# Two groups of fp32r rounding copies moved from VectorE to ScalarE in a fused attention, token-mixing and feed-forward kernel

## The chip, the cores and the metric

The kernel runs on one core of one Trainium2 chip. The metric is the device time of one execution in microseconds. Time zero of every view of the trace is the start of the span. TensorE multiplies (PE; PEld is its weight load), VectorE is DVE, ScalarE is ACT, GpSimd is POOL, SyncE is SP and issues nearly all DMAs.

## The reference, cut to what matters

```python
B, H, S, D, d_model, d_ff = 2, 8, 768, 64, 512, 1024
# attention with 8 global and 96 local keys and a linear bias, per batch and head
x = softmax(q k^T / sqrt(D) + bias) v              # to (B, S, 512)
# mixing
theta = x @ w_theta
zr, zi = x * cos(theta), x * sin(theta)
y = einsum('ts,bsd->btd', w_tok_r, zr) + einsum('ts,bsd->btd', w_tok_i, zi)
u = x + y
x2 = u + relu(u @ w_ch)
# feed-forward with a 3-tap convolution gate
h = relu(x2 @ w_in)
out = (h * sigmoid(conv(h, conv_w))) @ w_out
```

Weights come as fp64 and are converted on the chip.

## The kernel before, in words

**The numbers.** Products behind attention are made of three fp32r matmuls. Each operand is split into a rounded copy, `hi`, of type fp32r, and the remainder, `lo`, the operand minus `hi`; then hi × hi, lo × hi and hi × lo are added up in PSUM. `Net.hi(eng, out, in_)` (L99) makes the rounded copy: with "A" an activation of type Copy on ScalarE (L101), with "P" a copy on GpSimd, with anything else a copy on VectorE (L105). `Net.lo` (L107, row L109) subtracts, on VectorE unless told "P". So `lo` reads what `hi` wrote.

**Order of the work.** The schedule is written out by hand: each engine executes its instructions in the order in which the program issues them, and an instruction that waits holds all that is queued behind it on its engine.

**Attention** (`run_fast`, L799). The loop over j has 48 pairs of query tiles (16 heads of a batch, three pairs each) and 9 more rounds that drain it. In round j TensorE makes the scores of j, ScalarE the exponentials of j - 2 (L330), TensorE the transposes of j - 3 (L339), ScalarE their evacuation for j - 4 (L101, a<-PT), TensorE the product with v for j - 5, VectorE the softmax reduction of j - 1 (L321) and every third round the normalising of a head (L274 to L276). Every sixth round a column block c of x (four blocks of 128 per batch) is complete: `transpose_x` (L430) transposes it in two halves through the one bank X, and each half is copied to `xT` (on ScalarE, but on VectorE for the last block of batch 1). Three rounds later `split_xT` (L441) makes `xTs`: `hi` of 128x768 at the end of a round, `lo` in the next one. The last block of batch 1 is transposed and split at once, in round 54 (L861). A queue of small steps (`net.run`, weight conversion: L117 on ScalarE, L122 to L130 on VectorE, then `hi` on ScalarE and `lo` on VectorE) is worked off in the rounds.

**Theta.** theta of batch 0 (six tiles of 128 rows) is multiplied inside the attention loop by `theta_0`; `reduce_theta` (L473) reads a tile from its bank on ScalarE (L477, then L478), and VectorE takes off whole turns (L480). For batch 1 tiles 0 to 3 are opened in rounds 52, 54, 55 and 56 with column blocks 0 to 2 (`theta1_open`, L461; banks TH, S, S, PT). `tail` (L620) then adds block 3, and tiles 4 and 5 follow in banks TH and S (L656 to L658), that is, in the banks of tiles 0 and 1 once their reductions have read them.

**Trig.** `trig` (L482) turns a reduced theta tile into z in stages: on ScalarE an Abs and two Sin of 128x512 (L487 to L489); on VectorE two products with x (L493); then `hi` of both z and `lo` of both z (L495 to L498). The strings `em`, `eh`, `el` say on which engine products, `hi` and `lo` run; each has a letter for the real and one for the imaginary part. `trig0` (L501) runs the six tiles of batch 0 in a staggered way, one call per round from round 52 on: call k issues the first stage of tile k, the second of tile k - 1 and the third of tile k - 2, in that order. Calls 0 to 4 come in the loop. In `tail` come, in this order (L652): the reduction of theta tile 0 of batch 1 (L477, L478), call 5, the reduction of tile 1, L480 of tile 0, call 6, L480 of tile 1, then call 7:

```python
        red = [self.reduce_theta(th[t], r[t]) for t in range(2)]
        for chain in (red[0], early, red[1], red[0], early, red[1]):
            next(chain, None)
        for _ in early:
            pass
        th += [n.bank("TH"), n.bank("S", 2)]
        for t in (4, 5):
            self.theta_part(t, th[t], range(KC))
        reduce(th[2], r[2])
        reduce(th[3], r[3])
```

**Behind that** the token products of batch 0 start (`tok`, L525, 24 matmuls of 128x384 for each of the tiles s), first with z of tile 0. The trig tiles of batch 1 (L677) already use "AA" for `hi`. Then come the channel product, the feed-forward product with its gate, and the output product.

Of the kernel before, what the change touches and what calls it, by code (L numbers as in the profile page):

```python
# [407 lines left out]
class Mix:  # L408
# [32 lines left out]
    def split_xT(self, b, c, el="V"):  # L441
        n = self.net
        h, l = self.xTs
        n.hi("V", h[:, c], self.xT[b][:, c])
        yield
        n.lo(el, l[:, c], self.xT[b][:, c], h[:, c])

# [53 lines left out]
    def trig0(self):  # L501

        n = self.net
        z, tr = [[None, None] for _ in range(NT)], []
        self.z = [z, None]
        for k in range(NT + 2):
            if k == 1:
                zs = [n.slot(f"a{i}", [P, 3, 2, DM], F32R, "z") for i in range(4)]
                for i in range(2 * NT):
                    z[i // 2][i % 2] = zs[i // 3][:, i % 3]  # L510
            if k < NT:
                tr.append(self.trig(0, k, self.r[:, k], z[k], "VV", "VV", "VV"))
            for g in tr[max(0, k - 2) :][::-1]:
                next(g)
            yield
# [510 lines left out]
```

## Time and profile before

| | us |
|---|---|
| median of 3 runs | 418.61 |
| the 3 runs | 418.59, 418.61, 419.8 |
| the profiled execution | 418.75 |
| its span, first to last instruction | 416.5 |
| outside the span | 2.25 |

Durations and starts below are those of the profiled execution. A row of the timeline gives start, duration, engine, line, operation, output and inputs, count, and in brackets an idle wait ahead of it and what ended it. A row of the groups gives line, engine, operation, output and input, shape and type, count, then busy time and mean ns of one, then idle time ahead. Two instructions of one engine can overlap a little: the next one starts before the one ahead has ended.

### The profile page before, as it was taken

How to read it: one execution, taken by the hardware profiler on the slowest of the kernel's cores; microseconds unless marked ns; L12 is line 12 of the kernel's file. 1: busy time of each engine (PE TensorE's matmuls, PEld its weight loads, DVE VectorE, ACT ScalarE, POOL GpSimd, SP SyncE). 2: the span in 40 equal slices, each digit the busy share in tenths (PEclk: the TensorE clock that was granted, in tenths of full speed). 3: DMA queues.
4: the chain of work that ended last, by engine and by line, in shares of the span. 5: the costliest groups of instructions: out<-in, count | busy, mean ns of one | idle time of the engine just before them, and what ended most of it. 6: DMA issues, size and time to landing. Idle time of an engine off the chain costs nothing.

```text
span 416.5 us, 6402 instructions
## 1 busy us (share of the span) xinstructions
PE 403.7 (97%) x2376; PEld 379.2 (91%) x2376; DVE 318.4 (76%) x733; ACT 236.8 (57%) x449; POOL 4.4 (1%) x14
## 2 busy tenths in 40 slices
PE   4899999999999999999999999999999999999995
PEld 3899999988897899999999999999999998888885
DVE  4579999667568997899999999999699999800001
ACT  2777888685669536864436245446776889300000
POOL 4000000000000000000000000000000000000000
PEclk9999999999999999999999999999999999999999
DMA  6965776441420004006564352221000000111111
GB/s 168 255 177 178 214 226 161 123 131 35 142 84 2 0 9 144 2 1 188 178 202 155 101 169 84 63 91 52 0 2 0 2 0 0 53 49 50 52 50 58
DMA packets 13095, 38.03 MB, mean 91 GB/s; under 512 B 1856, under 2 KB 2304, under 8 KB 13056
## 3 DMA queue, kind: packets, MB, share of 16 engines
q1 hardware_dynamic: 12816, 37.13, 29.3%
q10 hardware_dynamic: 240, 0.41, 0.4%
q8 instruction: 20, 0.33, 0.3%
q14 instruction: 19, 0.16, 0.1%
HBM read 34.39 MB, written 3.15 MB: 90 GB/s over the span
## 4 chain that ended last, share of the span: by engine, by line
PE 95%; DMA 3%; DVE 1%; SPq 0%; issue 0%; DVEq 0%
PE O L112 26%; PE S L112 26%; PE PT L112 16%; PE TH L112 13%; PE X L112 9%; PE PT L339 4%; DMA qk<-qk 2%; PE X L437 1%; DMA words<-n 1%; SPq L258 0%; DVE a L321 0%; DVE xT L105 0%; SPq L224 0%; SPq L230 0%; DVE scratch L105 0%
## 5 line engine op out<-in xcount | busy, mean ns | idle before, releaser
L112 PE MATMUL S<-qk 128*128 128x256 f32 (+1 forms) x192 | 48.7, 380 | 7.4 <-DMA qk<-qk 7.2
L330 ACT ACTIVATE a<-a,nm 128x256 f32<-128x256 f32 (+1 forms) x96 | 41.5, 482 | 10.4 <-DVE nm L321 10.4
L321 DVE CUSTOM_DVE_ANT_0 a<-S,a 128x256 f32<-128x256 f32 (+1 forms) x96 | 34.5, 399 | 14.4 <-PE PT L339 12.3
L112 PEld LDWEIGHTS S<-qk 128*128 128x128 f32 x192 | 32.6, 198 | 11.1 <-issue 7.6
L101 ACT ACTIVATE a<-PT 128x512 f32<-128x512 f32 (+1 forms) x48 | 26.6, 554 | 11.2 <-PE PT L339 10.8
L112 PE MATMUL O<-a,a 128*128 128x65 f32 x236 | 29.8, 268 | 0.0
L112 PEld LDWEIGHTS O<-a,a 128*128 128x128 f32 x236 | 28.8, 192 | 0.0
L112 PE MATMUL PT<-wt,z 128*128 128x384 f32 x144 | 28.1, 335 | 0.0
L339 PE MATMUL PT<-ident,a 128*128 128x128 f32 x176 | 27.1, 273 | 0.0
L112 PE MATMUL O<-wt,z 128*128 128x384 f32 x144 | 26.9, 334 | 0.0
L339 PEld LDWEIGHTS PT<-ident,a 128*128 128x128 f32 x176 | 22.2, 141 | 4.5
L112 PE MATMUL S<-wt,z 128*128 128x384 f32 x144 | 26.2, 335 | 0.0
L101 ACT ACTIVATE wt<-wbit 128x384 fp32r<-128x384 f32 x24 | 12.5, 521 | 23.9 <-DVE wbit L130 23.9
L112 PE MATMUL TH<-wth,xTs 128*128 128x512 f32 x96 | 25.9, 406 | 0.0
L112 PEld LDWEIGHTS PT<-wt,z 128*128 128x128 f32 x144 | 25.3, 188 | 0.0
L112 PEld LDWEIGHTS O<-wt,z 128*128 128x128 f32 x144 | 25.2, 188 | 0.1
L112 PEld LDWEIGHTS S<-wt,z 128*128 128x128 f32 x144 | 25.2, 188 | 0.0
L117 ACT ACTIVATE wbit<-wst 128x384 f32<-128x384 f32 (+1 forms) x33 | 20.2, 612 | 3.3 <-DVE wout L109 1.1
L130 DVE SCALAR_TENSOR_TENSOR wbit<-wst,wbit 128x384 int32<-128x384 int32 (+1 forms) x33 | 20.6, 623 | 1.1
L129 DVE SCALAR_TENSOR_TENSOR wbit<-wst,wbit 128x384 int32<-128x384 int32 (+1 forms) x33 | 20.5, 622 | 0.9
L123 DVE TENSOR_SCALAR wbit<-wbit 128x512 int32<-128x512 int32 (+1 forms) x48 | 18.9, 394 | 1.6
L112 PEld LDWEIGHTS TH<-wth,xTs 128*128 128x128 f32 x96 | 17.1, 189 | 3.2
(180 smaller groups left out, 872.6 us busy)
## 6 DMA issues: line engine op xcount, KB each, us to landing
wst<-w_tok SPq DMA_DIRECT2D x17, 384.0 KB, 4.6
a<-v SPq DMA_DIRECT2D x16, 357.5 KB, 4.8
qk<-qk SPq DMA_DIRECT2D x14, 396.0 KB, 5.7
out<-scratch SPq DMA_DIRECT2D x11, 256.0 KB, 2.0
qk<-w_tok SPq DMA_DIRECT2D x7, 384.0 KB, 3.3
wst<-w_out SPq DMA_DIRECT2D x5, 512.0 KB, 3.4
wst<-w_theta SPq DMA_DIRECT2D x4, 512.0 KB, 7.6
qk<-w_in SPq DMA_DIRECT2D x4, 512.0 KB, 3.4
```

The costliest lines, as they stand in the source:

```text
L101: self.nc.scalar.activation(out, in_, AF.Copy)
L112: self.nc.tensor.matmul(out, l, r, start=start, stop=stop)
L117: self.nc.scalar.activation(t.bitcast(F32), w[:, 1 : w.shape[1] : 2].bitcast(F32), AF.Abs)
L123: nc.vector.tensor_scalar(t, t, 3, 0x3FFFFFFF, op0=ALU.logical_shift_left, op1=ALU.bitwise_and)
L129: nc.vector.scalar_tensor_tensor(t, lo, 29, t, op0=ALU.logical_shift_right, op1=ALU.bitwise_or)
L130: nc.vector.scalar_tensor_tensor(t, hi, -(1 << 30), t, op0=ALU.bitwise_and, op1=ALU.bitwise_or)
L321: nc.vector.tensor_tensor_reduce(sS[:, c], s["sp"][:, c], self.T[i % H][:, 256:TW] if t0 else self.T[i % H][:, 0:256], scale=-0.125, scala ...
L330: self.nc.scalar.activation(sS[:, rng[u]], sS[:, rng[u]], AF.Exp, bias=nm[:, u : u + 1], scale=-1.0)
L339: self.nc.tensor.transpose(pt[:, c], sS[:, c], net.head["ident"])
L437: self.nc.tensor.transpose(xb[:, P * jj : P * jj + P], self.xs[b][:, t, P * c : P * c + P], n.head["ident"])
```

## The change

The rounded copies of `xT` (8 of 128x768) and those of z of batch 0 (12 of 128x512) are issued on ScalarE instead of VectorE. The remainders stay on VectorE, and so does everything else; the order of issue is the same.

```diff
@@ -441,7 +441,7 @@
     def split_xT(self, b, c, el="V"):
         n = self.net
         h, l = self.xTs
-        n.hi("V", h[:, c], self.xT[b][:, c])
+        n.hi("A", h[:, c], self.xT[b][:, c])
         yield
         n.lo(el, l[:, c], self.xT[b][:, c], h[:, c])
 
@@ -509,7 +509,7 @@
                 for i in range(2 * NT):
                     z[i // 2][i % 2] = zs[i // 3][:, i % 3]
             if k < NT:
-                tr.append(self.trig(0, k, self.r[:, k], z[k], "VV", "VV", "VV"))
+                tr.append(self.trig(0, k, self.r[:, k], z[k], "VV", "AA", "VV"))
             for g in tr[max(0, k - 2) :][::-1]:
                 next(g)
             yield
```

## Rows read from the trace of the kernel before

**Rows 1.** The page's busy times and shares by engine.

```profile
PE 403.7 (97%) x2376; PEld 379.2 (91%) x2376; DVE 318.4 (76%) x733; ACT 236.8 (57%) x449; POOL 4.4 (1%) x14
```

**Rows 2.** Windows: stretch, length, busy time by engine, granted clock, DMA.

```profile
20.00:75.00 55.00, 54.85 (x416) 51.23 (x416) 50.72 (x185) 45.77 (x105) 0.00 (x0) 1.00 0.67 196
...
145.00:350.00 205.00, 205.00 (x1173) 204.19 (x1172) 192.41 (x341) 122.89 (x214) 0.00 (x0) 1.00 0.23 73
...
412.00:417.00 5.00, 0.00 (x0) 0.00 (x0) 0.22 (x1) 0.00 (x0) 0.00 (x0) 0.87 0.12 37
```

**Rows 3.** Groups by line: rounded copies on VectorE and on ScalarE.

```profile
L101 ACT ACTIVATE g<-c 128x768 fp32r<-128x768 f32 x16 | 13.3, 833 | 0.9 <-DVE c L597 0.9
...
L105 DVE CAST xTs<-xT 128x768 fp32r<-128x768 f32 x8 | 4.4, 554 | 0.0
...
L101 ACT ACTIVATE z<-r 128x512 fp32r<-128x512 f32 x6 | 3.7, 621 | 2.9 <-DVE r L493 2.9
...
L105 DVE CAST z<-r 128x512 fp32r<-128x512 f32 x6 | 2.5, 419 | 0.0
```

**Rows 4.** Timeline of ScalarE, 118 to 165 us.

```profile
120.65 0.60 ACT L101 ACTIVATE a<-PT 128x512 f32<-128x512 f32 x1 [0.22 <-PE PT L339]
121.56 0.91 ACT L330 ACTIVATE a<-a,nm 128x256 f32<-128x256 f32 x2 [0.31 <-DVE nm L321]
...
122.78 0.49 ACT L101 ACTIVATE xT<-X 128x384 f32<-128x384 f32 x1
...
125.38 0.62 ACT L487 ACTIVATE scratch<-r 128x512 f32<-128x512 f32 x1
126.01 1.28 ACT L488 ACT_TABLE_LOAD   x1
...
127.85 0.71 ACT L489 ACTIVATE scratch<-scratch,hp 128x512 f32<-128x512 f32 x1
128.46 0.62 ACT L487 ACTIVATE scratch<-r 128x512 f32<-128x512 f32 x1
...
135.04 0.71 ACT L489 ACTIVATE scratch<-scratch,hp 128x512 f32<-128x512 f32 x1
137.90 0.60 ACT L477 ACTIVATE r<-TH 128x512 f32<-128x512 f32 x1 [2.15 <-PE TH L112]
138.53 0.63 ACT L478 ACTIVATE scratch<-r 128x512 f32<-128x512 f32 x1
...
141.05 0.57 ACT L477 ACTIVATE r<-S 128x512 f32<-128x512 f32 x1
```

**Rows 5.** Timeline of TensorE, 118 to 165 us.

```profile
123.85 0.50 PE L437 MATMUL X<-ident,xs 128*128 128x128 f32 x3
...
130.31 0.55 PE L437 MATMUL X<-ident,xs 128*128 128x128 f32 x3 [0.65 <-DVE xT L105]
...
139.79 2.96 PE L112 MATMUL TH<-wth,xTs 128*128 128x512 f32 x12
142.59 2.96 PE L112 MATMUL S<-wth,xTs 128*128 128x512 f32 x12
```

**Rows 6.** Timeline of VectorE, 118 to 165 us.

```profile
128.72 0.69 DVE L493 TENSOR_TENSOR scratch<-scratch,xs 128x512 f32<-128x512 f32 x1
129.70 0.56 DVE L105 COPY xT<-X 128x384 f32<-128x384 f32 x1 [0.29 <-PE X L437]
130.90 0.56 DVE L105 COPY xT<-X 128x384 f32<-128x384 f32 x1 [0.64 <-PE X L437]
...
152.65 0.35 DVE L122 TENSOR_SCALAR wbit<-wbit 128x384 f32<-128x384 f32 x1
```

**Rows 7.** Timeline of ScalarE, 160 to 175 us: a pair of z of batch 1.

```profile
166.91 0.62 ACT L101 ACTIVATE z<-r 128x512 fp32r<-128x512 f32 x1
167.43 0.62 ACT L101 ACTIVATE z<-scratch 128x512 fp32r<-128x512 f32 x1
167.96 0.62 ACT L487 ACTIVATE scratch<-r 128x512 f32<-128x512 f32 x1
```

## The prediction

> **What bounds the kernel now.** I began with the busy shares of the page: TensorE 97%, VectorE 76%, ScalarE 57% [rows 1]. The shares say that ScalarE has room, but they are means over stages, so I went on to stretches of time. Between 145 and 350 us TensorE is busy for all 205 us [rows 2]: what delays its arrival at 145 delays the end by as much, because no gap behind it can give the time back. After that I read the three engines' timelines from 118 to 146 us, where attention ends, the early trig tiles of batch 0 run and the theta tiles of batch 1 are multiplied. The reader is to see there that ScalarE reaches the first theta reduction (L477, 137.90) after an idle wait of 2.15 us for TensorE [rows 4], and that TensorE goes from theta tile 4 (139.79) to theta tile 5 (142.59) without a gap [rows 5]. The one gap of TensorE is 0.65 us before the X transposes at 130.31, for a VectorE copy.
>
> **What moves, and its price.** VectorE loses 8 casts of 768 columns at 554 ns and 12 of 512 at 419 ns [rows 3], 9.5 us in all. On the bound that is worth at most the 0.65 us above. ScalarE gains as many copies. The same shapes and types run there already: 833 ns for 768 columns, 621 ns for 512 [rows 3]. Behind one another they start closer than that: two of 512 take 1.05 us from 166.91 to 167.96 [rows 7], which is 0.10 us less each than they last. So I count 0.73 us for a copy of 768 (0.833 less 0.10) and 1.05 us for a pair of 512. No DMA and no other queue is touched.
>
> The rows put VectorE ahead by a factor of 1.5. The Trainium skill (ScalarE: Activation LUTs, Rules for kernel authors) advises VectorE for simple element-wise operations, as up to about 3 times faster in bf16 on single-source operations. Three times VectorE's duration would be 1.26 us for a copy of 512, an estimate from that page; the four pairs counted below would add about 5 us more, and the sum would be about 427 us. The rows of this kernel's own fp32 copies decide, and the sum stays with them.
>
> **The four casts of x of batch 0** stand in the attention loop behind ScalarE's evacuation of a step. From 20 to 75 us ScalarE is busy 45.77 of 55 us [rows 2], so 9.2 us are free against 4 × 0.73 = 2.9 us. Exponentials and evacuations are issued a whole step of the loop ahead of the matmuls that read them, and the casts come six steps apart. I cost them at nothing; the cover is that step. If it failed, the price would be at most 2.9 us.
>
> **The first three casts of batch 1** fall between 119 and 126 us. Two come ahead of ScalarE's copy xT<-X at 122.78. That copy is preceded by waits of 0.22 and 0.31 us that the casts fill, and two starts that followed a wait now overlap by 0.10 us each: 2 × 0.73 - 0.53 - 0.20 = 0.73 us later, so it ends at 122.78 + 0.73 + 0.49 = 124.00. TensorE's second X transposes, at 123.85 before [rows 5], need that single bank and start at 124.04 (0.04 us is what one engine takes to follow another in these rows). That is 0.19 us lost, and ScalarE, whose last evacuation follows TensorE, comes free at 125.57 instead of 125.38 [rows 4]. The third cast takes it to 126.30.
>
> **The trig work, in order.** ScalarE's queue is strictly the program's order. The rows from 125.38 to 128.46 (3.08 us with the table load) are tile 0, and four more tiles follow to 135.65 (135.04 plus 0.71 less 0.10), 1.80 us each [rows 4]. After the change:
>
> tile 0 runs to 129.38 and tile 1 to 131.18. Now comes the fourth cast of batch 1, which needs both VectorE copies of X. The first of them stands behind the product of tile 0's second Sin. That Sin ended at 128.56 and ends 0.92 us later, at 129.48; the product, 0.69 us less 0.09, leads to a copy at 130.12 instead of 129.70 [rows 6], ended at 130.68. TensorE's X transposes go from 130.31 to 130.72, and the second copy from 130.90 to 131.31, ended at 131.87. The cast starts at 131.91: ScalarE, free at 131.18, stands for 0.73 us with all trig work queued behind it. Then: cast to 132.64, tile 2 to 134.44, rounded pair of tile 0 to 135.49, tile 3 to 137.29, pair of tile 1 to 138.34, tile 4 to 140.14, pair of tile 2 to 141.19. Each pair's products are done in time: VectorE waits for the pairs, not the reverse.
>
> **Where it reaches the bound.** The reduction L477 reads theta tile 0 out of bank TH, and theta tile 4 is written into that same bank. It starts at 141.19 instead of 137.90, lasts 0.60 us, and TensorE enters tile 4 at 141.83 instead of 139.79: 2.04 us late (0.41 us of it would have come from X anyway). Theta tile 5 takes an S bank that the next reduction (141.05 before [rows 4]) must empty. On ScalarE that one now stands behind L478 (0.63 + 0.53 us from the start of L477), the last trig tile (1.80) and the pair of tile 3 (1.05): 141.19 + 1.16 + 1.80 + 1.05 = 145.20. With 0.57 us for itself and 0.04 us, TensorE enters tile 5 at 145.81 instead of 142.59, **3.22 us late**.
>
> Behind that I add nothing. The token products need z of tile 0, whose rounded copies are made by 135.49; the later pairs have a tile of products each (24 matmuls at 205 us / 1173 [rows 2], 4.2 us of TensorE). VectorE's waits for z before the reductions go, and its weight conversion, which began at 152.65 [rows 6], starts near 152 with TensorE 3.2 us later: its slack grows.
>
> The sum against the profiled execution: 418.75 + 3.22 = 421.97 us. The median of the runs is 0.14 us lower, which gives 421.83. I predict 421.9 us.
>
> **Unknown sizes.** The wait of 0.73 us and the shift of 0.19 us hang on several handovers. At the low end both are nothing: 3.22 - 0.92 = 2.3 us, 421.0. At the high end copies do not overlap: four pairs at 1.24 instead of 1.05 and two casts at 0.83 instead of 0.73 add 0.96 us, for 422.9.
>
> **Rivals.** *First, hidden work, not slower:* L477 could start as late as 139.15 without holding TensorE (139.79 less 0.64), which is 3.50 us after ScalarE's trig work ends now. If less than that is added ahead of it, nothing is lost, and VectorE's lighter queue may return the 0.65 us before 130.31: 418.1 to 418.8 us. For it speaks ScalarE's 57% and the 2.15 us idle; against it, that I count 5.54 us of delay there (three pairs, 3.15; two casts, 1.46; the wait, 0.73; 0.19, rounded). It decides at 3.50.
>
> *Second, only the first bank counts:* if tile 5 found its S bank emptied, just the 2.04 us would stay: 420.8. Against it, the reduction at 141.05 is the one that frees that bank.
>
> *Third, the clock falls.* The granted clock is 1.00 through the busy stretches and has a mean of 0.87 only after the last matmul, when TensorE stands idle to the end [rows 2]; 0.65 us idle before 130.31 left no trace in it. The two stalls are 1.6 and 1.2 us with 2.8 us of matmuls between. If the 12 matmuls of tile 5 (2.80 us) then ran at the level of 1.2 GHz, that would cost 2.80 us more: 424.8. The Trainium skill (TensorE: Matmul & The Clock Gate, Why this matters for your kernels) says that a long enough idle gap between bursts of matmuls brings the half clock back. By that rule the gaps matter; the rows show a fall only after the end, so I give it little.
>
> *Fourth, no effect,* if the copies in fact stayed where they are or an unseen handover hid them: 418.7.
>
> **How the numbers follow.** Both banks late, 0.79; only the first bank, 0.07; clock, 0.05: all slower. Hidden work or no effect, 0.09, nearly all of it within 0.3%, since 0.65 us is 0.16%. A measurement of this kernel can tell about 0.3%, 1.26 us, from no change. So slower 0.91, same 0.07, faster 0.02. The range takes in the second rival and the bounds, with 0.3 us for runs that spread: 420.7 to 423.1.
>
> **What would show it.** Right: the copies of z and xTs stand on ScalarE; L477 for TH starts near 141; TensorE has an idle wait of about 1.6 us before theta tile 4 and of 1.2 us before tile 5, both released by ScalarE's L477; TensorE is without a gap behind; VectorE waits for ScalarE's z. Wrong: TensorE enters the token products before 147, or a new wait stands in attention or past 150, or the granted clock is below 1.00 after the stalls.

## The result, and the profile after

Seven runs of the changed kernel have a median of 421.6 us (421.23 to 424.38) against 418.75 us for seven of the kernel before. The ratio is 1.0071, 95% interval 1.0056 to 1.0087: **slower by 0.7%**, against 421.9 us predicted. The profiled execution took 421.94 us with a span of 419.7 us. One of the seven runs, at 424.38 us, had a mean granted clock of 0.993 where the others had 0.997 to 1.000; it left no trace, and the kernel before has runs like it in a later round (423.07 and 423.25 us at 0.990), so it is not put down to the change.

The page's busy times of the changed kernel, the line that answers to [rows 1]:

```profile
PE 404.7 (96%) x2376; PEld 379.5 (90%) x2376; DVE 311.6 (74%) x713; ACT 247.8 (59%) x469; POOL 4.4 (1%) x14
```

VectorE has lost its 20 casts and ScalarE has them (713 instead of 733 instructions, 469 instead of 449). TensorE's share is 96% instead of 97%; nothing else in these shares looks worse. The groups by line show that the copies cost what their models in [rows 3] cost:

```profile
L101 ACT ACTIVATE z<-r 128x512 fp32r<-128x512 f32 x12 | 7.4, 619 | 2.9 <-DVE r L493 2.9
L101 ACT ACTIVATE xTs<-xT 128x768 fp32r<-128x768 f32 x8 | 6.7, 836 | 0.6 <-DVE xT L105 0.6
```

The loss is seen in TensorE's timeline, 118 to 168 us (answering to [rows 5]):

```profile
123.73 0.55 PE L437 MATMUL X<-ident,xs 128*128 128x128 f32 x3
...
130.46 0.55 PE L437 MATMUL X<-ident,xs 128*128 128x128 f32 x3 [0.86 <-DVE xT L105]
...
141.55 3.07 PE L112 MATMUL TH<-wth,xTs 128*128 128x512 f32 x12 [1.44 <-ACT r L477]
145.53 3.08 PE L112 MATMUL S<-wth,xTs 128*128 128x512 f32 x12 [0.91 <-ACT r L477]
148.44 2.27 PE L112 MATMUL O<-wt,z 128*128 128x384 f32 x12
```

Two new waits stand ahead of theta tiles 4 and 5, and both end with ScalarE's L477, which reads the bank that TensorE is about to overwrite. The wait ahead of the second X transposes grew from 0.65 to 0.86 us. ScalarE's timeline in the same stretch (answering to [rows 4]) shows what stands in front of L477:

```profile
125.31 0.83 ACT L101 ACTIVATE xTs<-xT 128x768 fp32r<-128x768 f32 x1
...
131.64 0.85 ACT L101 ACTIVATE xTs<-xT 128x768 fp32r<-128x768 f32 x1 [0.63 <-DVE xT L105]
...
134.19 0.62 ACT L101 ACTIVATE z<-r 128x512 fp32r<-128x512 f32 x1
134.72 0.62 ACT L101 ACTIVATE z<-scratch 128x512 fp32r<-128x512 f32 x1
135.24 0.62 ACT L487 ACTIVATE scratch<-r 128x512 f32<-128x512 f32 x1
...
139.88 0.61 ACT L101 ACTIVATE z<-r 128x512 fp32r<-128x512 f32 x1
140.40 0.61 ACT L101 ACTIVATE z<-scratch 128x512 fp32r<-128x512 f32 x1
140.92 0.57 ACT L477 ACTIVATE r<-TH 128x512 f32<-128x512 f32 x1
...
144.90 0.57 ACT L477 ACTIVATE r<-S 128x512 f32<-128x512 f32 x1
```

From 125.31 to 144.90 ScalarE has one wait, the 0.63 us for the copy of X. The idle time of 2.15 us ahead of L477 [rows 4] is gone, and the engine with 59% of the span busy has become the one that TensorE waits for.

The granted clock is 1.00 through both waits, and behind 150 us TensorE has no gap, as before (windows: stretch, length, busy time by engine, granted clock, DMA):

```profile
140.00:145.00 5.00, 3.18 (x13) 2.18 (x12) 3.17 (x6) 4.94 (x10) 0.00 (x0) 1.00 0.00 0
145.00:150.00 5.00, 4.47 (x21) 3.92 (x22) 5.00 (x10) 4.91 (x10) 0.00 (x0) 1.00 0.00 0
150.00:353.00 203.00, 203.00 (x1163) 202.29 (x1162) 186.78 (x330) 121.67 (x212) 0.00 (x0) 1.00 0.24 74
```

### The profile page after: what moved, and what is told of

The parts are those of the page before. It is cut to its first block, busy times and chain, and to the rows that moved or that the text cites. A ratio compares the mean times of both kernels' runs of the same rounds, so it can differ in the third digit from the quotient of the medians.

```text
span 419.7 us, 6395 instructions
## 1 busy us (share of the span) xinstructions
PE 404.7 (96%) x2376; PEld 379.5 (90%) x2376; DVE 311.6 (74%) x713; ACT 247.8 (59%) x469; POOL 4.4 (1%) x14
## 3 DMA queue, kind: packets, MB, share of 16 engines
HBM read 34.39 MB, written 3.15 MB: 89 GB/s over the span
## 4 chain that ended last, share of the span: by engine, by line
PE 90%; ACT 4%; DMA 3%; DVE 1%; issue 1%; SPq 0%; DVEq 0%; ACTq 0%
PE O L112 25%; PE S L112 24%; PE PT L112 15%; PE TH L112 11%; PE X L112 9%; PE PT L339 4%; DMA qk<-qk 2%; PE X L437 1%; ACT z L101 1%; ACT scratch L489 1%; ACT scratch L487 1%; DMA words<-n 1%; ACT xTs L101 0%; ACT r L488 0%; ACT L488 0%
```

## The experiments

The theory: only time in ScalarE's queue ahead of the two reductions counts, and only beyond the room: 3.50 us ahead of the first, and by the same sum 3.37 us ahead of the second (142.59 - 0.61 = 141.98, less 135.65 and the 1.16 and 1.80 us that stood there already). Rival A: each moved copy costs by itself. Rival B: VectorE, which now waits for copies made elsewhere, is late. Where nothing else is said, a diff is against the changed kernel.

### Each part alone

The copies of z only:

```diff
-        n.hi("A", h[:, c], self.xT[b][:, c])
+        n.hi("V", h[:, c], self.xT[b][:, c])
```

> Only the rounded copies of z of batch 0 go to ScalarE; those of xTs stay on VectorE. Theory (ScalarE's queue ahead of the two reductions that free the banks): trig work ends 3 pairs later, 135.65 + 3.15 = 138.80, so L477 for bank TH begins 0.35 us before the 139.15 from which it would hold TensorE: no stall before theta tile 4. L477 for the S bank begins at 138.80 + 1.16 + 1.80 + 1.05 = 142.81 and ends with its handover at 143.42 instead of 142.59: one stall of 0.83 us, total 418.75 + 0.83 = 419.6 us. Rival A (each moved copy costs by itself, through its longer duration or a handover): about 12/20 of the 2.9 us, 420.5. Rival B (VectorE, waiting for ScalarE's copies, is what is late): the whole loss of z stays, 421 or more.

The copies of xTs only:

```diff
-                tr.append(self.trig(0, k, self.r[:, k], z[k], "VV", "AA", "VV"))
+                tr.append(self.trig(0, k, self.r[:, k], z[k], "VV", "VV", "VV"))
```

> Only the rounded copies of xTs go to ScalarE; those of z stay on VectorE. Theory: two casts and one wait for the copy of X, about 2.4 us, fit in front of L477 (3.50 us), so there is no stall before theta tiles 4 and 5; the gap before the second X transposes grows from 0.65 to about 0.85 us with a small slip before it, 0.1 to 0.4 us lost, and attention gains up to 0.4 us between 52 and 55 us where VectorE's casts were in the way: 418.5 to 419.0 us. Rival A (each moved copy costs by itself): about 8/20 of the 2.9 us, 419.9. The two parts alone then add up to about 0.8 us where the whole change lost 2.9.

Measured beside the kernel before (419.27 us, the median of 29 runs): z only 420.23 us, ratio 1.0028 (0.9999 to 1.0057); xTs only 418.88 us, ratio 0.9988 (0.9970 to 1.0006). The kernel before is 0.5 us slower here than the 418.75 us that the expectations start from, and the runs scatter by about as much as is asked, so the traces decide. TensorE's timeline of z only and ScalarE's reductions there:

```profile
139.99 2.96 PE L112 MATMUL TH<-wth,xTs 128*128 128x512 f32 x12
143.59 3.08 PE L112 MATMUL S<-wth,xTs 128*128 128x512 f32 x12 [0.64 <-ACT r L477]
```

```profile
138.98 0.57 ACT L477 ACTIVATE r<-TH 128x512 f32<-128x512 f32 x1
142.96 0.57 ACT L477 ACTIVATE r<-S 128x512 f32<-128x512 f32 x1
```

As the theory had it, there is no wait before tile 4 and one before tile 5. Counted from the first theta matmul of batch 0 (77.19 here, 77.02 before), tile 5 starts at 66.40 instead of 65.57: **0.83 us late, the figure expected** (4.20 us of pairs less 3.37). With xTs only, neither tile waits (TensorE's timeline):

```profile
130.24 0.55 PE L437 MATMUL X<-ident,xs 128*128 128x128 f32 x3 [0.86 <-DVE xT L105]
...
139.73 2.96 PE L112 MATMUL TH<-wth,xTs 128*128 128x512 f32 x12
142.53 2.96 PE L112 MATMUL S<-wth,xTs 128*128 128x512 f32 x12
```

So the parts cost 0.92 and 0.36 us from the first theta matmul to the start of the last output products, 1.28 together, and the whole change costs 3.26 (table below). Rival A, a price for each copy, can't give that. Both parts draw on the same room.

### The same copies, in another order

```diff
-        for k in range(NT + 2):
+        steps = ((0,), (1, 0), (2, 1, 0), (3, 2), (4, 3), (1,), (5, 4, 2), (5, 3), (4,), (5,))
+        for k, step in enumerate(steps):
...
-        for chain in (red[0], early, red[1], red[0], early, red[1]):
+        for chain in (red[0], early, red[0], red[1], early, red[1], red[0], early, red[1]):
```

Here call k advances the tiles that `step` lists by one stage each, and the reduction is cut in three: L477, then L478, then L480 (the two ScalarE lines are 485 and 488 in this file).

> All 20 copies on ScalarE as in the change, but the order of issue at the end of attention is altered: pairs of tiles 1 and 2 come behind the first L477, and L477 of the second tile comes ahead of the last trig tile. Theory (only the place in ScalarE's queue costs): L477 for TH begins near 139.1 and ends before TensorE asks (about 140.2); the second L477 begins near 141.3, ends before 142.6: no stall before either theta tile, total 418.4 to 419.1 us, as fast as before with the same copies on the same engine. Rival A (the copies cost by themselves on ScalarE) and rival B (VectorE waits for them): 421 to 422 us as in the changed kernel.

Measured: 418.97 us, ratio 1.0002 (0.9976 to 1.0028), where the changed kernel has 1.0071. ScalarE's timeline and TensorE's:

```profile
138.85 0.58 ACT L485 ACTIVATE r<-TH 128x512 f32<-128x512 f32 x1
139.32 0.62 ACT L101 ACTIVATE z<-r 128x512 fp32r<-128x512 f32 x1
139.84 0.63 ACT L101 ACTIVATE z<-scratch 128x512 fp32r<-128x512 f32 x1
140.37 0.62 ACT L488 ACTIVATE scratch<-r 128x512 f32<-128x512 f32 x1
140.88 0.59 ACT L485 ACTIVATE r<-S 128x512 f32<-128x512 f32 x1
```

```profile
139.96 2.96 PE L112 MATMUL TH<-wth,xTs 128*128 128x512 f32 x12
142.76 2.96 PE L112 MATMUL S<-wth,xTs 128*128 128x512 f32 x12
145.56 2.27 PE L112 MATMUL O<-wt,z 128*128 128x384 f32 x12
```

All 20 copies are on ScalarE, and the loss is gone: of the 3.26 us behind the first theta matmul 0.37 are left (table below), as much as the xTs copies alone cost. VectorE still waits for ScalarE's z, 5.7 us over the whole span against 5.1 in the changed kernel (waits: us in total, times, longest; the changed kernel, then this run):

```profile
DVE z L109 <- ACT z L101: 5.1, 8, 1.6
DVE z L109 <- ACT z L101: 5.7, 7, 1.6
```

This run decides against rivals A and B: what costs is the place of the copies in the queue.

### More time in the same place

```diff
         for i, s in ((1, r), (0, a)):
-            n.hi(eh[i], z[i][:, 0], s)
+            for _ in range(2 if b == 0 else 1):
+                n.hi(eh[i], z[i][:, 0], s)
```

> As the change, but each rounded copy of z of batch 0 is issued twice on ScalarE (same source, same target). Theory: three more pairs ahead of the first L477 and a fourth ahead of the second add 3 x 1.05 + 1.05 = 4.2 us to the start of theta tile 5: 421.6 + 4.2 = 425.8 us, with 3.15 us of it before theta tile 4. Rival A (the loss comes from a fixed handover for each of the tiles, not from time in the queue): under 1 us more, 422 to 422.5. Rival B (VectorE is late): the remainders are issued as often as before, 2 us more at most.

Measured: 427.6 us, ratio 1.0182 (1.0148 to 1.0217), against 425.8 expected. The queue explains it, with another price. A pair issued twice takes 2.37 us on ScalarE (139.04 to 141.41 below), not 2.10: two copies from the same source to the same target did not overlap. ScalarE's timeline:

```profile
139.04 1.28 ACT L101 ACTIVATE z<-r 128x512 fp32r<-128x512 f32 x2
140.23 1.28 ACT L101 ACTIVATE z<-scratch 128x512 fp32r<-128x512 f32 x2
141.41 0.61 ACT L487 ACTIVATE scratch<-r 128x512 f32<-128x512 f32 x1
```

That is 1.32 us more for a pair: 3.96 us for the three ahead of tile 4, 5.28 for the four ahead of tile 5. In TensorE's timeline, counted from the first theta matmul (77.50), the two tiles start at 68.70 and 74.00 where the changed kernel has 64.74 and 68.72: later by 3.96 and 5.28. A fixed handover (under 1 us more) and a late VectorE (at most 2 us more) do not give that.

```profile
146.20 5.43 PE L112 MATMUL TH<-wth,xTs 128*128 128x512 f32 x12 [5.40 <-ACT r L477]
151.50 3.07 PE L112 MATMUL S<-wth,xTs 128*128 128x512 f32 x12
```

```profile
145.00:150.00 5.00, 3.80 (x9) 3.03 (x10) 2.28 (x5) 4.87 (x10) 0.00 (x0) 0.50 0.00 0
```

Tile 4 itself took 5.30 us instead of 2.80, at a granted clock of 0.50 (the window above); it ended just as the second reduction did (150.87 + 0.58), so this cost nothing here.

### Time on ScalarE with no copy moved

The kernel before, with 6 or 10 extra copies of 512 columns ahead of the first reduction:

```diff
+        for _ in range(6):
+            n.hi("A", e[:, 0:DM], r[5])
         red = [self.reduce_theta(th[t], r[t]) for t in range(2)]
```

> The kernel before, with 6 extra 512-column copies on ScalarE ahead of the first L477 (their target is overwritten later; nothing reads them); no copy is moved and VectorE's work is the same. Theory: 6 x 0.525 = 3.15 us is under the 3.50 us of room, L477 begins at 138.80 instead of 137.90 and TensorE goes from theta tile 3 to 4 to 5 without a gap: 0 to 0.2 us slower than before. Rival A (ScalarE time in that stretch costs in proportion): 1.5 us or more slower.

> As the one with 6, but 10 extra copies, 5.25 us on ScalarE. Theory: over the room of 3.50 us by 1.75: L477 begins at 140.90, theta tile 4 at 141.54 (1.75 us late), theta tile 5 at 144.47 (1.88 us late), total 1.9 us over the kernel before, with no change at all in which engine makes which copy. Rival B (the loss of the change comes from VectorE waiting for copies made elsewhere): no loss, since VectorE waits for none of these.

Measured beside the kernel before (419.0 us, the median of 26 runs): 419.58 us with 6, ratio 1.0016 (1.0005 to 1.0027), and 423.9 us with 10, ratio 1.0099 (1.0076 to 1.0122). ScalarE's timeline with 6 and TensorE's wait:

```profile
135.20 3.94 ACT L101 ACTIVATE z<-r 128x512 fp32r<-128x512 f32 x6
139.05 0.58 ACT L477 ACTIVATE r<-TH 128x512 f32<-128x512 f32 x1
```

```profile
139.68 3.07 PE L112 MATMUL TH<-wth,xTs 128*128 128x512 f32 x12 [0.18 <-ACT r L477]
```

Six copies from one source to one target take 3.85 us (135.20 to 139.05), not 3.15, again without overlap. That is 0.35 over the room of 3.50, and tile 4 starts 0.35 us late (63.12 from the first theta matmul at 76.56, against 62.77). Tiles 4 and 5 then take 2.95 and 2.91 us instead of 2.80, which accounts for the rest of the 0.59 us in the table. So the loss is above the 0 to 0.2 us expected, since the price was too low, but far below rival A's 1.5, and the room of 3.50 us is confirmed to within what the trace resolves.

With 10 copies (ScalarE, then TensorE):

```profile
137.01 6.59 ACT L101 ACTIVATE z<-r 128x512 fp32r<-128x512 f32 x10
143.51 0.58 ACT L477 ACTIVATE r<-TH 128x512 f32<-128x512 f32 x1
```

```profile
144.14 4.61 PE L112 MATMUL TH<-wth,xTs 128*128 128x512 f32 x12 [2.83 <-ACT r L477]
148.59 2.96 PE L112 MATMUL S<-wth,xTs 128*128 128x512 f32 x12
```

6.50 us, not the 5.25 expected, is 3.00 over the room, and tile 4 starts 3.00 us late (65.77 against 62.77). Rival B had no loss here. The expected 1.9 us was far too little: besides the price it left out the clock. Tile 4 took 4.45 us instead of 2.80, 1.65 more (together 4.65; the table has 4.61, the medians 4.9), and the windows show a granted clock of 0.68 from 145 to 150 us:

```profile
145.00:150.00 5.00, 5.00 (x17) 3.95 (x16) 5.00 (x11) 4.24 (x8) 0.00 (x0) 0.68 0.00 0
```

### The part that helps, and a version faster than both

```diff
-        n.hi("A", h[:, c], self.xT[b][:, c])
+        n.hi("V" if b else "A", h[:, c], self.xT[b][:, c])
...
-                tr.append(self.trig(0, k, self.r[:, k], z[k], "VV", "AA", "VV"))
+                tr.append(self.trig(0, k, self.r[:, k], z[k], "VV", "VV", "VV"))
```

> Only the four rounded copies of xTs of batch 0, inside attention, go to ScalarE; everything else stays as before. Theory: ScalarE has room there, so nothing is lost; VectorE is relieved where it held back a bank of scores, so TensorE's gap near 53 us goes and 0.2 to 0.4 us is gained: 0.05 to 0.1% under the kernel before, within what can be measured. Rival A (each moved copy costs by itself): 4/20 of the loss, 0.6 us slower. The X gap at 130 stays 0.65 us.

In addition, in the round that transposes the last block of x:

```diff
-            for chain in (mix.transpose_x(1, KC - 1, "V"), mix.split_xT(1, KC - 1, "V")):
+            tx = mix.transpose_x(1, KC - 1, "V")
+            next(tx)
+            mix.theta1_open(1)
+            next(tx)
+            next(early)
+            for chain in (tx, mix.split_xT(1, KC - 1, "V")):
...
-        if j in OPEN:
+        if j in OPEN and j != NJ + 6:
...
-        if j >= NJ + 4:
+        if j >= NJ + 4 and j != NJ + 6:
```

> The four casts of batch 0 on ScalarE as in the one before, all others on VectorE; in addition the two halves of the last X transposes are issued with the opening of theta tile 1 between them, and the trig call of that round ahead of the second copy of X. Theory: TensorE's gap of 0.65 us before the second X transposes goes, and so does the small one near 53 us: 0.9 to 1.1 us under the kernel before, 0.2 to 0.25%, with no gap of TensorE from 17 us to the end. Rival: the later second copy makes xTs late for the last part of theta tile 0, or the reduction late for the S bank, and a new gap takes the place of the old one: same as before or slower.

Measured: the four casts alone 418.99 us, ratio 0.9989 (0.9976 to 1.0002), within what can be measured, as expected. With the order of the X transposes altered, 417.3 us, ratio 0.9963 (0.9950 to 0.9976): **faster than the kernel before by more than the interval**, and so than the changed kernel. It is more than the 0.25% expected, which lies just inside the interval; the table below has 0.38 and 0.87 us, 1.25 or 0.3%. TensorE's timeline shows the transposes between the two theta openings without a wait, and its windows no idle time from 20 to 405 us (one of them behind the rows):

```profile
128.56 0.49 PE L437 MATMUL X<-ident,xs 128*128 128x128 f32 x3
128.80 2.34 PE L112 MATMUL S<-wth,xTs 128*128 128x512 f32 x9
130.98 0.49 PE L437 MATMUL X<-ident,xs 128*128 128x128 f32 x3
...
125.00:135.00 10.00, 10.00 (x55) 8.41 (x54) 8.90 (x17) 9.85 (x16) 0.00 (x0) 1.00 0.01 2
```

### All kernels by two stretches of TensorE

Times from the traces, in us. "Attention" runs from the second set of X transposes near 32 us to the first theta matmul of batch 0; "rest" from there to the start of the last group of output products.

| kernel | attention | rest | rest against before |
|---|---|---|---|
| before | 44.64 | 332.36 | |
| changed | 44.26 | 335.62 | +3.26 |
| z only | 44.66 | 333.28 | +0.92 |
| xTs only | 44.26 | 332.72 | +0.36 |
| all copies, other order | 44.26 | 332.73 | +0.37 |
| pairs twice | 44.26 | 340.90 | +8.54 |
| xTs of batch 0 only | 44.26 | 332.36 | 0.00 |
| 6 extra copies | 44.64 | 332.95 | +0.59 |
| 10 extra copies | 44.64 | 336.97 | +4.61 |
| xTs of batch 0, X transposes apart | 44.26 | 331.49 | -0.87 |

Attention takes 44.26 us wherever the casts of batch 0 are on ScalarE, and 44.64 or 44.66 wherever they are on VectorE.

## Why the prediction was right, point by point

**The price of the copies** (0.73 us for 768 columns, 1.05 for a pair of 512): right; the fourth cast stands from 131.64 to 132.39, 0.75 us apart, and a pair from 134.19 to 135.24, 1.05 us.

**The two stalls.** From the first theta matmul (76.81 after, 77.02 before), theta tile 4 starts 1.97 us later and tile 5 3.15 us later; the prediction had 2.04 and 3.22. On the same count L477 starts at 64.11 and 68.09, where the predicted 141.19 and 145.20 are 64.17 and 68.18. The small difference for tile 4 comes from ahead of the trig work: the X transposes slipped by 0.09 us instead of 0.19 (they start at 46.92 on that count, 46.83 before), and ScalarE begins that work 0.87 us late instead of 0.92. From the fourth cast to the first L477 the queue takes 9.28 us in the sum (131.91 to 141.19) and in the trace (131.64 to 140.92). The wait for the copy of X is 0.63 us in its row, counted from the end of the instruction ahead (131.01); counted as in the prediction, from where a start could have followed 0.10 us earlier, it is the predicted 0.73. Likewise the rows give waits of 1.44 and 0.91 us where the prediction named about 1.6 and 1.2: from the point at which tile 4 or 5 would have started without a wait (139.95 and 144.35), they are 1.60 and 1.18. Of the lateness of tile 4, X was to bring 0.41 us; the run with the xTs copies alone has 0.36 in all. The step as a whole, the queue ahead of the two reductions, is shown by the reordered kernel and by the extra copies.

**Two terms that I did not have.** The first is a gain: "on the bound that is worth at most the 0.65 us" overlooked a small wait inside attention, of which the 54.85 of 55 us of TensorE in [rows 2] were a sign. In the kernel before, TensorE's weight loads have it, for a softmax reduction of VectorE that had not yet emptied a bank of scores (timeline of the weight loads, 52 to 55 us):

```profile
53.64 0.52 PEld L112 LDWEIGHTS S<-qk 128*128 128x128 f32 x4 [0.28 <-DVE nm L321]
```

The changed kernel has no such row, and attention takes 0.38 us less; the run with the four casts alone shows that they are the cause. Counted from the second X transposes, the matmuls of that group start at 21.26 us in the kernel before and at 20.96 in that run, which is 0.30 of the 0.38 us. I had costed these four casts at nothing, having looked for harm only. The second is a loss: a theta tile that follows a wait takes 2.91 us, not 2.80 (145.53 to 148.44). Its weights are then loaded after the wait instead of ahead of it, as the weight loads of the changed kernel show, at 141.54 and 145.53 together with the matmuls, where without a wait they come 0.22 us earlier (142.37 for 142.59 in the kernel before). That the late weight load is the cause is a reading of these rows, which the extra copies bear out: with 6, tile 5 has a wait in its weight loads alone (0.32 us) and takes 2.91 us; with 10, its weights come 0.23 us ahead and it takes 2.79.

```profile
141.54 2.64 PEld L112 LDWEIGHTS TH<-wth,xTs 128*128 128x128 f32 x12 [1.87 <-ACT r L477]
145.53 2.65 PEld L112 LDWEIGHTS S<-wth,xTs 128*128 128x128 f32 x12 [1.35 <-ACT r L477]
```

With these the whole is 3.15 + 0.11 = 3.26, less 0.38, 2.88 us; the medians differ by 2.85.

**The rivals.** Hidden work would have needed less than 3.50 us ahead of L477; the prediction counted 5.54 there, and the trace has 5.48. The point from which it decides was right: the runs with xTs only (no stall), with z only (none at tile 4) and with 6 extra copies (0.35 us over, 0.35 us late) bracket it. The second rival fell with the wait before tile 5. The falling clock did not show in the changed kernel's profile, whose windows have 1.00 through both stalls; it is real, though, as the runs with longer stalls show (0.50 and 0.68 over 145 to 150 us).

**The price of a copy by rule and by row.** The rule of the Trainium skill (ScalarE: Activation LUTs, Rules for kernel authors) that prefers VectorE for simple operations pointed the right way here, but not by its quantity: the rows have a factor of 1.5 (833 to 554 ns, 621 to 419) in place of up to about 3, and the same copies at the same price on ScalarE lost nothing in another order. The Trainium skill (Perfetto Trace Analysis, Optimizing Scalar/DVE Operations) also says that offloading work from VectorE to ScalarE may make sense if VectorE is saturated. The runs agree with that inside attention, 0.38 us gained with VectorE at 50.72 of 55 us [rows 2], and not behind it, from 135 to 150 us, where VectorE was busy 5.00 of every 5 us in the kernel before but TensorE waited for none of its work.

## What to carry to other kernels

Before moving work to an engine with room, find what stands behind it in that engine's queue and who waits for that: here it was the read that frees a PSUM bank, and 0.7% was lost on an engine that is busy 59% of the time. Room in front of such an instruction is one budget that all moved work shares, so parts that cost little alone can cost much together; work it out from the timeline as the latest start that holds nobody. If the work has to be on that engine, issue the bank-freeing read first.

## What the runs showed that I had not expected

**The clock after a stall.** Where TensorE stood idle 5.40 us (pairs twice) the granted clock fell to 0.50, the lower of its two levels, and 12 matmuls took 5.30 us instead of 2.80; after 2.83 us idle (10 extra copies) they took 4.45. The six runs with 10 extra copies range from 422.06 us at a mean granted clock of 0.997 to 424.75 us at 0.994; only the last left a trace, so whether the clock fell in each of them stays open. After the changed kernel's 1.44 and 0.91 us the profile shows no fall.

**Repeated copies don't overlap on ScalarE.** Ten in a row from one source to one target took 6.50 us, 0.65 each, where a pair with two sources and two targets takes 0.525 each. The rows of the kernel before show the same for an instruction that reads what the one ahead of it wrote: L478 starts 0.63 us after L477, which lasts 0.60 [rows 4]. Whether the source or the target holds the copies back, no run separates. It made three of my expectations too small (3.15 us for six was 3.85, 5.25 for ten was 6.50, 4.2 for four repeated pairs was 5.28).
